# Splitting two more products of a polyphase convolution into half-width matmuls, with a staged third group

## The chip, the cores and the metric

One core of a Trainium2 chip. The metric is the time of one execution on the device in microseconds; the kernel before takes 896.56 us (median of 4 runs, 895.82 to 897.54). Its executions agree within some 0.3%. Differences of medians of 2 to 3 us are readable where the runs lie side by side, and smaller ones hardly.

## The reference

```python
# x (2, 4000, 512), w (15, 512, 1024), w_o (512, 512), all bf16
dil = 2; pad = (K - 1) * dil
xp = jnp.pad(x, ((0, 0), (pad, 0), (0, 0)))
h = sum(jnp.einsum('btc,cd->btd', xp[:, pad - i*dil : pad - i*dil + T, :], w[i]) for i in range(K))
z = jnp.tanh(h[..., :D]) * sigmoid(h[..., D:])
return z @ w_o
```
(The sum is written out as a loop there.) It is a causal convolution over time with 15 taps two steps apart, a gate, and an output projection.

## The kernel before

Time is cut into eight interleaved phases; four phases of one parity of one batch form a *supertile*. With three-multiplication tricks, nested, the convolution between four phases needs nine products (a, b, c, d, e, f, g, hh, ii) in place of sixteen; sums of inputs (U02 = U0 + U2 and so on) and sums of weights go in, sums and differences of the products come out. A *unit* is all nine products for one block of 128 output columns, one supertile and one half (tanh or sigmoid): 4 passes x 4 supertiles x 2 halves = 32 units. Only the first pass transposes and sums the inputs; it also writes them to DRAM, from where the later passes load them. Weights are summed anew for every pass. Work for later units (loads, sums, spills to DRAM) is attached to the products as *hooks*: a hook is issued behind the product whose index it carries.

A whole product is 16 matmuls of 501 columns (e has 12: a tap is missing). A *split* product applies the trick once more, along time: three groups of 8 matmuls of 251 columns.

```python
SPLIT = ("a", "c", "d", "f", "g", "ii")
...
wsl_pool:  bufs=33 + 2 * NSPL + 2      # weight slabs: 47 buffers
xin_pool:  bufs=(9 - NSPL) + 4         # natural inputs: 7
xh_pool:   bufs=NSPL                   # inputs in halves (odd "o", "m", "n"): 6
pcopy_pool 2, ctmp_pool 2, keep_pool 4, hpre_pool 2   # fp32 tiles of 501 columns
z_pool 6;  hsb_pool 2;  ps_pool 8 PSUM banks
...
def product(pn):                       # whole: 16 matmuls, N = 501, into one PSUM bank
    ...
def split_product(pn, dst):
    ps_o = ps_pool.tile([P, NH1], f32, ...)
    half_mms(ps_o, slabs2[pn], xt[n + "o"], True)              # group o: pair sums of weights
    u_h = hsb_pool.tile([P, NH1], f32, ...)
    nc.scalar.copy(u_h[:, :], ps_o[:, :])                      # must come before group m
    ps_e = ps_pool.tile([P, NH1], f32, ...)
    half_mms(ps_e, [sl[0], sl[2]], xt[n + "n"], True)          # group e
    V.tensor_tensor(dst[:, 1:NP1:2], ps_e[:, 1:NH1], u_h[:, 0:NKH], ALU.add)
    half_mms(ps_o, [sl[1], sl[3]], xt[n + "m"], False)         # group m, accumulates on ps_o
    nc.scalar.copy(dst[:, 0:NP1:2], ps_o[:, :])
...
def produce_halves(n):                 # first pass only
    nc.scalar.copy(to, nat[:, :, base + 1:base + 2 * XH:2])
    nc.scalar.copy(tm, nat[:, :, base:base + 2 * XH - 1:2])
    nc.gpsimd.memset(tn[:, :, 0:1], 0.0)
    sum_eng.tensor_tensor(tn[:, :, 1:XH], tm[:, :, 1:XH], to[:, :, 0:XH - 1], ALU.subtract)
    sum_eng.tensor_tensor(tm, tm, to, ALU.subtract)
...
for pi, pn in enumerate(PRODS):        # emit_unit
    if pn == "a":
        r["a_sb"] = to_sbuf("a", "a_sb")                       # split_product
    elif pn == "b":
        ps = product(pn)
        V.tensor_tensor(p1[:, K1], r["a_sb"][:, K1], ps[:, KSH], ALU.add)
        V.tensor_tensor(q1[:, K1], r["a_sb"][:, K1], ps[:, K1], ALU.add)
    ...                                # c .. ii in the same manner, act_out() for tanh, sigmoid
    for h in hooks.get(pi, []):        # loads, sums and spills for later units
        h()
...
# last unit: output projections as hooks (6, steps[0]), (7, steps[2]); steps[1], steps[3] after it
# zld_pool (loads of z for the output projection) 6, osb_pool 5
# weights of the next pass: half 0 in the last unit of a pass, half 1 in the first of the next
```

u_h is copied by ScalarE from the bank on which group m accumulates, so TensorE can't start group m before the copy is done.

## Time and profile before

| | before |
|---|---|
| time, median | 896.56 us; profiled span 894.3 us |
| matmuls, TensorE's granted clock | 6336, 0.998 |
| VectorE, ScalarE busy | 530.0 us (59%), 303.4 us (34%) |
| moved by DMA | 145.66 MB |
| one plain unit | 25.0 us |

The lines behind it stand in the prediction. Read them by the *starts* of TensorE's groups: what a pipelined engine takes for a group is the distance to the next start, not the duration printed beside it.

### The profile page before, as it was taken

The page shows a single profiled execution, that of the slowest core. Times are in us where ns is not written, and L with a number is a line of the kernel's source. Part 1 is how long each engine was busy: PE and PEld are TensorE (multiplying, and loading weights), DVE is VectorE, ACT ScalarE, POOL GpSimd, SP SyncE. Part 2 cuts the span into 40 slices and gives each one's busy share as a digit, 9 for nine tenths or more (in the row PEclk, how much of TensorE's full clock was granted, in tenths as well). Part 3 has the DMA queues.
Part 4 walks back from the last instruction along what each step waited for, and adds up shares of the span by engine and source line. Part 5 has one row for each costly group of instructions (what it writes and reads, how often), then busy time and mean ns, then how long its engine had stood idle before and what let it go on. Part 6 is the DMA issues. An engine that isn't in the chain of part 4 may idle for free.

```text
span 894.3 us, 16197 instructions
## 1 busy us (share of the span) xinstructions
PE 873.0 (98%) x6336; PEld 617.5 (69%) x6336; DVE 530.0 (59%) x1058; ACT 303.4 (34%) x625; POOL 27.7 (3%) x76
## 2 busy tenths in 40 slices
PE   6889999999999999999999999999999999999998
PEld 3356777777777777777777777777776676776674
DVE  3999596776975454455975454455974145244352
ACT  4435353632222222222222222222223423424334
POOL 8200000000000000000000000000000000000000
PEclk9999999999999999999999999999999999999999
DMA  9976656566948081636848081636937435435304
GB/s 226 314 196 232 143 196 171 174 231 171 240 131 248 14 251 40 203 102 177 237 127 264 15 249 42 202 103 177 243 105 239 135 119 179 121 105 167 99 2 126
DMA packets 138024, 145.66 MB, mean 163 GB/s; under 512 B 77276, under 2 KB 124700, under 8 KB 137948
## 3 DMA queue, kind: packets, MB, share of 16 engines
q1 hardware_dynamic: 136508, 140.70, 53.6%
q0 software_dynamic: 1440, 3.93, 1.7%
q8 instruction: 49, 0.80, 0.4%
q14 instruction: 27, 0.22, 0.1%
HBM read 99.25 MB, written 39.26 MB: 155 GB/s over the span
## 4 chain that ended last, share of the span: by engine, by line
PE 84%; DVE 10%; DMA 2%; issue 1%; ACT 1%; POOL 1%; SPq 0%; DVEq 0%; ACTq 0%; POOLq 0%
PE ps_b L341 11%; PE ps_hh L341 10%; PE ps_e L341 8%; PE po L481 6%; PE ps_c_o L354 6%; PE ps_d_o L354 6%; PE ps_f_o L354 5%; PE ps_a_o L354 5%; PE ps_ii_o L354 5%; PE ps_g_o L354 5%; PE ps_d_e L354 3%; PE ps_f_e L354 3%; PE ps_c_e L354 3%; PE ps_ii_e L354 3%; PE ps_g_e L354 3%; PE ps_a_e L354 3%
## 5 line engine op out<-in xcount | busy, mean ns | idle before, releaser
L341 PEld LDWEIGHTS <-wo_p 128*128 128x128 bf16 x1060 | 102.9, 97 | 110.0 <-issue 1.3
L354 PEld LDWEIGHTS <-wo_p 128*128 128x128 bf16 x1116 | 108.3, 97 | 16.7 <-issue 3.7
L341 PE MATMUL ps_b<-xU,wo_p 128*128 128x501 bf16 x512 | 113.8, 374 | 0.0
L341 PE MATMUL ps_e<-xU,wo_p 128*128 128x501 bf16 x384 | 86.9, 375 | 0.0
L341 PE MATMUL ps_hh<-xU,whh_p 128*128 128x501 bf16 x384 | 86.7, 375 | 0.0
L354 PEld LDWEIGHTS <-wii_p 128*128 128x128 bf16 x744 | 72.3, 97 | 16.9 <-issue 2.0
L354 PEld LDWEIGHTS <-wc_p 128*128 128x128 bf16 x744 | 72.1, 97 | 15.4 <-issue 0.3
L354 PEld LDWEIGHTS <-wg_p 128*128 128x128 bf16 x744 | 72.2, 97 | 9.0
L409 DVE TENSOR_TENSOR p<-a_sb,ps_b 128x500 f32<-128x500 f32 x32 | 21.6, 676 | 82.2 <-PE ps_b L341 81.8
L354 PEld LDWEIGHTS <-wf_p 128*128 128x128 bf16 x620 | 60.2, 97 | 13.6
L424 DVE TENSOR_TENSOR p<-d_sb,ps_e 128x500 f32<-128x500 f32 x32 | 21.6, 675 | 80.4 <-PE ps_e L341 76.0
L354 PE MATMUL ps_ii_o<-xU0123h,wii_p 128*128 128x251 bf16 x496 | 64.0, 271 | 1.8 <-ACT u_h L369 1.8
L354 PE MATMUL ps_c_o<-xU02h,wc_p 128*128 128x251 bf16 x496 | 64.0, 271 | 0.2 <-ACT u_h L369 0.2
L354 PE MATMUL ps_g_o<-xU01h,wg_p 128*128 128x251 bf16 x496 | 63.9, 271 | 0.0
L341 PEld LDWEIGHTS <-whh_p 128*128 128x128 bf16 x384 | 37.2, 97 | 38.2 <-DVE whh_p L164 0.4
L382 ACT ACTIVATE th<-H 128x500 bf16<-128x500 f32 x64 | 39.3, 620 | 50.4 <-DVE H L453 19.5
L386 ACT ACTIVATE sg<-H 128x500 bf16<-128x500 f32 x64 | 39.0, 620 | 37.9 <-DVE H L453 15.0
L481 PE MATMUL po<-wo_sb,zl 128*126 128x512 bf16 (+1 forms) x192 | 51.9, 379 | 0.0
L354 PE MATMUL ps_f_o<-xU13h,wf_p 128*128 128x251 bf16 x372 | 50.5, 271 | 0.0
L489 ACT CAST o_sb<-po 128x512 bf16<-128x512 f32 (+1 forms) x64 | 37.4, 586 | 32.6 <-PE po L481 29.3
L449 DVE TENSOR_TENSOR C<-g_sb,ps_hh 128x500 f32<-128x500 f32 x32 | 21.6, 674 | 44.6 <-PE ps_hh L341 44.5
L369 ACT COPY u_h<-ps_ii_o 128x251 f32<-128x251 f32 x31 | 11.4, 368 | 93.4 <-PE ps_ii_o L354 93.4
(122 smaller groups left out, 1253.5 us busy)
## 6 DMA issues: line engine op xcount, KB each, us to landing
xU<-xsp_U SPq DMA_DIRECT2D x36, 516.0 KB
wo_p<-in_w_dram SPq DMA_DIRECT2D x90, 128.0 KB
xU0h<-xsp_U0h SPq DMA_DIRECT2D x12, 756.0 KB
xU02h<-xsp_U02h SPq DMA_DIRECT2D x12, 756.0 KB
xU1h<-xsp_U1h SPq DMA_DIRECT2D x12, 756.0 KB
xU13h<-xsp_U13h SPq DMA_DIRECT2D x12, 756.0 KB
xU01h<-xsp_U01h SPq DMA_DIRECT2D x12, 756.0 KB
xU0123h<-xsp_U0123h SPq DMA_DIRECT2D x12, 756.0 KB
```

Source lines behind the costliest of these rows:

```text
L341: nc.tensor.matmul(ps[:, :], lhsT=slabs[pn][l][:, cc, hcols], rhs=xtile[:, cc, st:st + NP1], start=(idx == 0), stop=(idx == len(mm) - 1),)
L354: nc.tensor.matmul(ps[:, :], lhsT=taps[lam][:, cc, hcols], rhs=xtile[:, cc, st:st + NH1], start=(first and idx == 0), stop=(idx == len(mm) ...
L369: nc.scalar.copy(u_h[:, :], ps_o[:, :])
L382: nc.scalar.activation(th[:], H[:, K1], AF.Tanh)
L386: nc.scalar.activation(sg[:], H[:, K1], AF.Sigmoid)
L409: V.tensor_tensor(r["p1"][:, K1], r["a_sb"][:, K1], ps[:, KSH], ALU.add)
L424: V.tensor_tensor(r["p2"][:, K1], r["d_sb"][:, K1], ps[:, KSH], ALU.add)
L449: V.tensor_tensor(r["C0"][:, K1], r["g_sb"][:, K1], ps[:, KSH], ALU.add)
L481: nc.tensor.matmul(po[:ksz, :], lhsT=zs[dcp][:, k0:k0 + ksz], rhs=wo_sb[:, dcp, :], start=(dcp == 0), stop=(dcp == HC - 1),)
L489: nc.scalar.copy(o_sb[:ksz, :], po[:ksz, :])
```

## The change

The intent: b and hh are split as well (only e stays whole), so that each gives up a quarter of its matmul columns. Two products used to be read straight from PSUM and now become SBUF tiles; tiles are reused in place and pools shrink so that all fits. And the split is staged: group m of a product is issued after groups o and e of the next one, so that TensorE has work while ScalarE copies u_h.

```diff
-    SPLIT = ("a", "c", "d", "f", "g", "ii")
+    SPLIT = ("a", "b", "c", "d", "f", "g", "hh", "ii")
-    wsl_pool = ... bufs=33 + 2 * NSPL + 2          # 47
+    wsl_pool = ... bufs=33 + 2 * NSPL + 0          # 49, for 49 tiles
     xin_pool = ... bufs=(9 - NSPL) + 4             # 7 -> 5
     xh_pool = ... bufs=NSPL                        # 6 -> 8
-    pcopy 2, ctmp 2, keep 4, hpre 2, z 6
+    lng 3, sht 5, z 4                              # combinations in place
...
-        def split_product(pn, dst):
+        def split_stage_a(pn, dst):                # groups o and e, u_h, first addition
             ...
+            return ps_o
+        def split_stage_b(pn, dst, ps_o):          # group m and its copy
             half_mms(ps_o, [sl[1], sl[3]], xt[n + "m"], False)
             nc.scalar.copy(dst[:, 0:NP1:2], ps_o[:, :])
...
+        stage_a(PRODS[0])
+        for pi in range(1, NPR):
+            stage_a(PRODS[pi])
+            stage_b(pi - 1, PRODS[pi - 1])         # combinations and hooks are in stage_b
+        stage_b(NPR - 1, PRODS[NPR - 1])
...
-    xnat_pool = ... bufs=11                        # natural rows for the transposes
+    xnat_pool = ... bufs=9
+    WLEAD = 2                                      # two weight steps ahead of the first unit, not one
...
-            zld_pool bufs=6, osb_pool bufs=5
+            zld_pool bufs=5, osb_pool bufs=4
...                                                 # weights of the next pass, spread:
-                            add_hook(pi, nwsteps[0][pi])
-                        deferred_g = nwsteps[1]
+                            if pi < 5:
+                                add_hook(pi, nwsteps[0][pi])
+                        deferred_g = nwsteps       # the rest over the first two units of the next pass
...                                                 # last unit:
-                        add_hook(6, steps[0])
-                        add_hook(7, steps[2])
-                        pending_outproj = [steps[1], steps[3]]
+                        add_hook(5, steps[0])
+                        add_hook(6, steps[2])
+                        add_hook(7, steps[1])
+                        pending_outproj = [steps[3]]
```
(The schedule of input sums in the first pass, PROD_SCHED and HALF_SCHED, also moves: U23 is made earlier, U2 and U23 get their halves. In the first pass the last four weight steps of the second half also move, from the end of the first unit into the second.)

More of the change, by code (lines that the diff above doesn't have):

```diff
@@ L95 @@
     dram = ctx.enter_context(tc.tile_pool(name="dram", bufs=1, space=DRAM))
-    wsl_pool = ctx.enter_context(tc.tile_pool(name="wsl", bufs=33 + 2 * NSPL + 2))
+    wsl_pool = ctx.enter_context(tc.tile_pool(name="wsl", bufs=33 + 2 * NSPL + 0))
     xin_pool = ctx.enter_context(tc.tile_pool(name="xin", bufs=(9 - NSPL) + 4))
     xh_pool = ctx.enter_context(tc.tile_pool(name="xh", bufs=NSPL + XH_SPARE)) if NSPL else None
-    pcopy_pool = ctx.enter_context(tc.tile_pool(name="pcopy", bufs=2))
     hsb_pool = ctx.enter_context(tc.tile_pool(name="hsb", bufs=2)) if NSPL else None
-    ctmp_pool = ctx.enter_context(tc.tile_pool(name="ctmp", bufs=2))
-    keep_pool = ctx.enter_context(tc.tile_pool(name="keep", bufs=4))
-    hpre_pool = ctx.enter_context(tc.tile_pool(name="hpre", bufs=2))
+    lng_pool = ctx.enter_context(tc.tile_pool(name="lng", bufs=3))
+    sht_pool = ctx.enter_context(tc.tile_pool(name="sht", bufs=5))
     th_pool = ctx.enter_context(tc.tile_pool(name="th", bufs=4))
     sg_pool = ctx.enter_context(tc.tile_pool(name="sg", bufs=2))
-    z_pool = ctx.enter_context(tc.tile_pool(name="z", bufs=6))
+    z_pool = ctx.enter_context(tc.tile_pool(name="z", bufs=4))
     ps_pool = ctx.enter_context(tc.tile_pool(name="ps", bufs=8, space=PSUM))
@@ L372, in split_product @@
             V.tensor_tensor(dst[:, 1:NP1:2], ps_e[:, 1:NH1], u_h[:, 0:NKH], ALU.add)
+            return ps_o
+        def split_stage_b(pn, dst, ps_o):
+            n = XNAME[pn]
+            sl = slabs[pn]
             half_mms(ps_o, [sl[1], sl[3]], xt[n + "m"], False)
@@ L391, in act_out, with stage_a @@
                     nc.sync.dma_start(zsp[(dc, b, p, q)][:], zt[:])
-        def to_sbuf(pn, nm):
-            t = ftile(pcopy_pool, nm)
-            if pn in SPLIT and use_split:
-                split_product(pn, t)
+        SBUF_PRODS = {"a": sht_pool, "c": lng_pool, "d": sht_pool, "f": sht_pool, "g": lng_pool,
+                      "ii": sht_pool}
+        r = {}
+        pend = {}
+        def stage_a(pn):
+            is_split = pn in SPLIT and use_split
+            pool = SBUF_PRODS.get(pn, sht_pool if is_split else None)
+            if pool is None:
+                r[pn] = product(pn)
+                return
+            t = ftile(pool, pn + "_sb")
+            r[pn] = t
+            if is_split:
+                pend[pn] = split_stage_a(pn, t)
             else:
@@ L399, in to_sbuf @@
                 nc.scalar.copy(t[:, ALLC], ps[:, ALLC])
-            return t
-        r = {}
-        for pi, pn in enumerate(PRODS):
-            if pn == "a":
-                r["a_sb"] = to_sbuf("a", "a_sb")
-            elif pn == "b":
-                ps = product(pn)
-                r["p1"] = ftile(keep_pool, "p1")
-                V.tensor_tensor(r["p1"][:, K1], r["a_sb"][:, K1], ps[:, KSH], ALU.add)
-                r["q1"] = ftile(ctmp_pool, "q1")
-                V.tensor_tensor(r["q1"][:, K1], r["a_sb"][:, K1], ps[:, K1], ALU.add)
-            elif pn == "c":
-                if "c" in SPLIT and use_split:
-                    ps = to_sbuf("c", "c_sb")
-                else:
-                    ps = product(pn)
-                r["A1"] = ftile(keep_pool, "A1")
-                V.tensor_tensor(r["A1"][:, K1], ps[:, K1], r["q1"][:, K1], ALU.subtract)
-            elif pn == "d":
-                r["d_sb"] = to_sbuf("d", "d_sb")
-            elif pn == "e":
-                ps = product(pn)
-                r["p2"] = ftile(keep_pool, "p2")
-                V.tensor_tensor(r["p2"][:, K1], r["d_sb"][:, K1], ps[:, KSH], ALU.add)
-                r["q2"] = ftile(ctmp_pool, "q2")
-                V.tensor_tensor(r["q2"][:, ALLC], r["d_sb"][:, ALLC], ps[:, ALLC], ALU.add)
-            elif pn == "f":
-                if "f" in SPLIT and use_split:
-                    ps = to_sbuf("f", "f_sb")
-                else:
-                    ps = product(pn)
-                r["B1"] = ftile(keep_pool, "B1")
-                V.tensor_tensor(r["B1"][:, ALLC], ps[:, ALLC], r["q2"][:, ALLC], ALU.subtract)
-                H0 = ftile(hpre_pool, "H0")
-                V.tensor_tensor(H0[:, K1], r["p1"][:, K1], r["B1"][:, KSH], ALU.add)
@@ new lines, in stage_b @@
+        def stage_b(pi, pn):
+            if pn in pend:
+                split_stage_b(pn, r[pn], pend.pop(pn))
+            if pn == "b":
+                r["p1"] = ftile(lng_pool, "p1")
+                V.tensor_tensor(r["p1"][:, K1], r["a"][:, K1], r["b"][:, KSH], ALU.add)
+                V.tensor_tensor(r["a"][:, K1], r["a"][:, K1], r["b"][:, K1], ALU.add)
+            elif pn == "c":
+                V.tensor_tensor(r["c"][:, K1], r["c"][:, K1], r["a"][:, K1], ALU.subtract)
+            elif pn == "e":
+                r["p2"] = ftile(sht_pool, "p2")
+                V.tensor_tensor(r["p2"][:, K1], r["d"][:, K1], r["e"][:, KSH], ALU.add)
+                V.tensor_tensor(r["d"][:, ALLC], r["d"][:, ALLC], r["e"][:, ALLC], ALU.add)
+            elif pn == "f":
+                V.tensor_tensor(r["f"][:, ALLC], r["f"][:, ALLC], r["d"][:, ALLC], ALU.subtract)
+                H0 = ftile(sht_pool, "H0")
+                V.tensor_tensor(H0[:, K1], r["p1"][:, K1], r["f"][:, KSH], ALU.add)
@@ L436, in emit_unit @@
                 act_out(0, H0)
-                H2 = ftile(hpre_pool, "H2")
-                V.tensor_tensor(H2[:, K1], r["A1"][:, K1], r["p2"][:, K1], ALU.add)
-                act_out(2, H2)
                 V.tensor_tensor(r["p1"][:, K1], r["p1"][:, K1], r["p2"][:, K1], ALU.add)
-                r["s"] = r["p1"]
-                V.tensor_tensor(r["A1"][:, K1], r["A1"][:, K1], r["B1"][:, K1], ALU.add)
-                r["s3"] = r["A1"]
-            elif pn == "g":
-                r["g_sb"] = to_sbuf("g", "g_sb")
-            elif pn == "hh":
-                ps = product(pn)
-                r["C0"] = ftile(ctmp_pool, "C0")
-                V.tensor_tensor(r["C0"][:, K1], r["g_sb"][:, K1], ps[:, KSH], ALU.add)
-                r["qg"] = ftile(ctmp_pool, "qg")
-                V.tensor_tensor(r["qg"][:, K1], r["g_sb"][:, K1], ps[:, K1], ALU.add)
-                H1 = ftile(hpre_pool, "H1")
-                V.tensor_tensor(H1[:, K1], r["C0"][:, K1], r["s"][:, K1], ALU.subtract)
-                act_out(1, H1)
-            elif pn == "ii":
-                if "ii" in SPLIT and use_split:
-                    ps = to_sbuf("ii", "ii_sb")
-                else:
-                    ps = product(pn)
-                r["C1"] = ftile(ctmp_pool, "C1")
-                V.tensor_tensor(r["C1"][:, K1], ps[:, K1], r["qg"][:, K1], ALU.subtract)
-                H3 = ftile(hpre_pool, "H3")
-                V.tensor_tensor(H3[:, K1], r["C1"][:, K1], r["s3"][:, K1], ALU.subtract)
-                act_out(3, H3)
@@ new lines, in stage_b @@
+                V.tensor_tensor(r["p2"][:, K1], r["c"][:, K1], r["p2"][:, K1], ALU.add)
+                act_out(2, r["p2"])
+                V.tensor_tensor(r["c"][:, K1], r["c"][:, K1], r["f"][:, K1], ALU.add)
+            elif pn == "hh":
+                C0 = ftile(sht_pool, "C0")
+                V.tensor_tensor(C0[:, K1], r["g"][:, K1], r["hh"][:, KSH], ALU.add)
+                V.tensor_tensor(r["g"][:, K1], r["g"][:, K1], r["hh"][:, K1], ALU.add)
+                V.tensor_tensor(C0[:, K1], C0[:, K1], r["p1"][:, K1], ALU.subtract)
+                act_out(1, C0)
+            elif pn == "ii":
+                V.tensor_tensor(r["ii"][:, K1], r["ii"][:, K1], r["g"][:, K1], ALU.subtract)
+                V.tensor_tensor(r["ii"][:, K1], r["ii"][:, K1], r["c"][:, K1], ALU.subtract)
+                act_out(3, r["ii"])
@@ L494 @@
     USE_DMAT = True
-    PROD_SCHED = [(0, "U0"), (0, "U2"), (0, "U1"), (0, "U3"), (4, "U02"), (5, "U13"), (6, "U01"),
-                  (7, "U23"), (8, "U0123")]
-    HALF_SCHED = [(4, "U0"), (5, "U02"), (5, "U1"), (6, "U13"), (7, "U01"), (8, "U0123")]
+    PROD_SCHED = [(0, "U0"), (0, "U2"), (0, "U1"), (0, "U3"), (4, "U02"), (4, "U23"), (5, "U13"),
+                  (6, "U01"), (8, "U0123")]
+    HALF_SCHED = [(4, "U0"), (4, "U2"), (5, "U02"), (5, "U1"), (6, "U13"), (7, "U01"), (8, "U23"),
+                  (8, "U0123")]
     HALF_SCHED = [(pi, n) for (pi, n) in HALF_SCHED if n in XSPLIT]
@@ L501 @@
     es0 = ExitStack()
-    xnat_pool = es0.enter_context(tc.tile_pool(name="xnat", bufs=11))
+    xnat_pool = es0.enter_context(tc.tile_pool(name="xnat", bufs=9))
     wts, wsteps = make_weight_steps(0, nc.vector, nc.gpsimd, defer_pairs=True)
@@ L507 @@
     XLEAD = 2
+    WLEAD = 2
     for pi in range(XLEAD):
         xsteps[pi]()
-    wsteps[0][0]()
+    for pi in range(WLEAD):
+        wsteps[0][pi]()
     deferred_g = None
@@ L517 @@
             nc.sync.dma_start(wo_sb[:], w_o.rearrange("(dc p) e -> p dc e", p=P))
-            zld_pool = ctx.enter_context(tc.tile_pool(name="zld", bufs=6))
-            osb_pool = ctx.enter_context(tc.tile_pool(name="osb", bufs=5))
+            zld_pool = ctx.enter_context(tc.tile_pool(name="zld", bufs=5))
+            osb_pool = ctx.enter_context(tc.tile_pool(name="osb", bufs=4))
         pending_outproj = []
@@ L536 @@
                             add_hook(pi, xsteps[pi + XLEAD])
-                        if pi + 1 < NPR:
-                            add_hook(pi, wsteps[0][pi + 1])
+                        if pi + WLEAD < NPR:
+                            add_hook(pi, wsteps[0][pi + WLEAD])
                         if pi >= GLAG:
                             add_hook(pi, wsteps[1][pi - GLAG])
+                if dc == 0 and si == 0 and hf == 1:
                     for pj in range(NPR - GLAG, NPR):
-                        add_hook(NPR - 1, wsteps[1][pj])
+                        add_hook(pj - (NPR - GLAG), wsteps[1][pj])
                 if hf == 0 and dc == 0:
@@ L575 @@
                             add_hook(pi, nxs["steps"][pi])
-                            add_hook(pi, nwsteps[0][pi])
-                        deferred_g = nwsteps[1]
+                            if pi < 5:
+                                add_hook(pi, nwsteps[0][pi])
+                        deferred_g = nwsteps
                     else:
                         steps = make_outproj_steps(b, p, state["z"])
-                        add_hook(6, steps[0])
-                        add_hook(7, steps[2])
-                        pending_outproj = [steps[1], steps[3]]
+                        add_hook(5, steps[0])
+                        add_hook(6, steps[2])
+                        add_hook(7, steps[1])
+                        pending_outproj = [steps[3]]
                 if hf == 0 and si == 0 and dc > 0 and deferred_g is not None:
-                    for pi in range(NPR):
-                        add_hook(pi, deferred_g[pi])
-                    deferred_g = None
+                    for pi in range(5, NPR):
+                        add_hook(pi - 5, deferred_g[0][pi])
+                    for pi in range(5):
+                        add_hook(pi + 4, deferred_g[1][pi])
+                    late_g, deferred_g = deferred_g[1], None
+                if hf == 1 and si == 0 and dc > 0:
+                    for pi in range(5, NPR):
+                        add_hook(pi - 5, late_g[pi])
                 if last_pass and hf == 0 and pending_outproj:
```

## The prediction

> **What bounds the kernel now.** I read the page first, then the TensorE timeline of one plain unit, then what TensorE waited for, then the busy times unit by unit. A unit is one pass over the nine products a, b, c, d, e, f, g, hh, ii for one 128-column block, one supertile and one half (tanh or sigmoid); there are 4 x 4 x 2 = 32 of them. The page:
>
> ```profile
> PE 873.0 (98%) x6336; PEld 617.5 (69%) x6336; DVE 530.0 (59%) x1058; ACT 303.4 (34%) x625; POOL 27.7 (3%) x76
> PEclk9999999999999999999999999999999999999999
> ...
> PE 84%; DVE 10%; DMA 2%; issue 1%; ACT 1%; POOL 1%; SPq 0%; DVEq 0%; ACTq 0%; POOLq 0%
> ```
>
> TensorE is busy nearly always, at full clock, and is 84% of the chain that ended last. Busy time of a pipelined engine proves little, so I look at starts. The TensorE timeline of one unit:
>
> ```profile
> 462.03 3.56 PE L341 MATMUL ps_b<-xU,wo_p 128*128 128x501 bf16 x16
> 465.43 1.03 PE L354 MATMUL ps_c_o<-xU02h,wc_p 128*128 128x251 bf16 x8
> 466.30 1.03 PE L354 MATMUL ps_c_e<-xU02h,wc_p 128*128 128x251 bf16 x8
> 467.17 1.03 PE L354 MATMUL ps_c_o<-xU02h,wc_p 128*128 128x251 bf16 x8
> 468.04 1.03 PE L354 MATMUL ps_d_o<-xU1h,wd_p 128*128 128x251 bf16 x8
> ...
> 478.41 2.71 PE L341 MATMUL ps_hh<-xU,whh_p 128*128 128x501 bf16 x12
> 480.96 1.01 PE L341 MATMUL ps_hh<-xU,wo_p 128*128 128x501 bf16 x4
> 481.80 1.03 PE L354 MATMUL ps_ii_o<-xU0123h,wii_p 128*128 128x251 bf16 x8
> ```
>
> Each row starts where the one before has issued its last matmul. A whole product b takes 465.43 - 462.03 = 3.40 us (16 matmuls, 212 ns each); hh takes 481.80 - 478.41 = 3.39 us. A split product takes 468.04 - 465.43 = 2.61 us (24 half-width matmuls, 109 ns each). The windows view, cut at unit boundaries (columns: window, length, busy time of PE, PEld, DVE, ACT and POOL):
>
> ```profile
> 11.00:52.40 41.40, 35.43 (x176) 15.69 (x174) 36.08 (x75) 17.24 (x22) 14.75 (x25) 0.96 1.04 293
> 52.40:77.40 25.00, 24.97 (x198) 17.87 (x197) 23.55 (x53) 13.86 (x22) 0.73 (x6) 1.00 0.53 159
> 77.40:105.50 28.10, 26.16 (x199) 19.01 (x197) 20.76 (x36) 11.16 (x22) 0.66 (x5) 1.00 0.79 212
> ...
> 308.20:333.20 25.00, 25.00 (x190) 18.26 (x189) 12.47 (x23) 6.83 (x17) 0.00 (x0) 1.00 0.69 213
> 433.20:458.20 25.00, 25.00 (x191) 18.27 (x189) 25.00 (x66) 6.58 (x16) 0.00 (x0) 1.00 0.72 197
> ```
>
> A plain unit is 25.0 us = 6 x 2.61 + 2 x 3.40 + 2.55 (e, 12 matmuls), so it is the matmul stream and nothing else; VectorE and ScalarE are half idle beside it. Two kinds of units are different: the first one (41.4 us) and the first of each later pass (433.2 here), where VectorE is busy all 25.0 us with weight sums, yet TensorE keeps its pace. All that TensorE waited for in the whole run is 17 us:
>
> ```profile
> PE pt L231 <- DMA xn<-in_x_dram: 7.2, 4, 3.3
> PE ps_ii L341 <- DVE wii_p L164: 3.1, 1, 3.1
> PE ps_g L341 <- DVE wg_p L164: 2.8, 3, 1.7
> PE ps_a_o L354 <- ACT u_h L369: 2.1, 3, 1.1
> PE ps_ii_o L354 <- ACT u_h L369: 1.8, 1, 1.8
> ```
>
> So the time is the sum of matmul columns plus some 17 us, most of it in the first unit.
>
> **What the Trainium skill says.** "TensorE: Matmul & The Clock Gate", section Back-to-back issue gap, gives N/2.4 + 2.5 ns for a warm matmul: 107 ns for 251 columns and 211 ns for 501. The trace has 109 and 212, so it agrees; the same section's sustained figure of about 131 ns for N=512 does not fit this trace. What matters: a half-width matmul really costs half, and the weight loads (97 ns each, 69% of the span) stay under it. The page's section Part 2 says that only weight loads are pulled ahead and matmuls stay in program order, so one matmul that waits for ScalarE stops all; the five u_h waits above agree. "VectorE: DVE Perf Modes", section The TRN2 errata, gives (N+151)/0.96 ns for an fp32 tensor_tensor, 678 ns at N=500. The trace has 676 ns with one operand in PSUM and 679 with both in SBUF, so moving b and hh to SBUF should not change the cost of the combining additions.
>
> **The change part by part.**
> 1. Products b and hh are split like the six others: 16 matmuls of 501 columns become 24 of 251. 3.40 - 2.61 = 0.79 us each, twice a unit, in 31 units (the first unit doesn't split): 31 x 2 x 0.79 = 49.0 us off the stream. All of it lies on the path.
> 2. In exchange each of the 62 new splits adds two ScalarE copies (368 and some 385 ns) and one VectorE addition (0.41 us): 47 us of ScalarE, 25 us of VectorE. Per plain unit VectorE goes to some 13.3 of 23.4 us, ScalarE to some 8.4. Beside the stream; nothing on the path.
> 3. Inputs U2 and U23 now get halves: per supertile four ScalarE copies of 1.04 us and four VectorE subtractions of 0.68 us, all in the first pass (16.6 and 10.9 us in total). Weight pair sums rise by 8 a pass, from 60 to 68 VectorE operations of about 0.36 us: 12 us over the run. VectorE in total: 530 + 25 + 11 + 12 = 578 us, 68% of the new span. ScalarE: 303 + 47 + 17 = 367 us, 43%.
> 4. Loads and spills of the two inputs grow from 516 to 756 KB, in 12 loads and 4 spills each: 16 x 2 x 0.24 = 7.7 MB on 145.66 MB. The mean goes from 163 to some 181 GB/s; slices of the page reach 314. Hidden.
> 5. Staging: the third group of a split product now runs after the first two groups of the next product. That gives the u_h copy one more product, some 1.7 us of slack. The u_h waits are 2.1 + 1.8 + 0.2 = 4.1 us; I expect nearly all to go.
> 6. The weight sums of a pass are spread. By my count of the additions, before, some 16, 41 and 3 fall into the last unit of the old pass and the first two of the new; after, 12, 34 and 22. The unit with 34 has 13.3 + 34 x 0.36 = 25.5 us of VectorE work in 23.4, so VectorE falls some 2 us behind and carries that on. Two u_h buffers and eight PSUM banks absorb about 6 us (the third group of a product comes 7.8 us after its first copy two products earlier, less 1.5 us of copy and addition). The weight pool has no spare buffer left, so sums and loads wait for the product that frees one, some 2.6 us each, in a lightly loaded unit. I allow 1 us for all of this and for the smaller output-projection pools.
> 7. Start-up. Before the second supertile begins to run freely (105.5 us), VectorE is busy 81 us; I add 5.4 for halves, 3 for pair sums, 1.6 for additions. The natural input pool shrinks from 7 to 5 buffers, and the first unit uses all nine natural tiles: U01 can only be made when U13 is freed by product f, so g waits for at least one 1.23 us sum. Against it, the new order asks for one input step less ahead of each product. I put the net at 4 us longer.
> Sum: 896.6 - 49.0 - 4.1 + 1 + 4 = 848.5; I say 848.
>
> **The rivals.** (A) VectorE becomes the bound in some units, the first three and the first of each pass. For it: 25.00 of 25.00 us busy at 433.2, 36.08 of 41.40 in the first unit. Against it: TensorE didn't slow at all at 433.2, and the sums are now spread. It would give back 3 us per pass change and 6 to 10 at the start, so 855 to 865. (B) The removed buffers take the place of the wait: input, weight and combine tiles turn over later, and transfers on the one queue sit behind a wait for a buffer. For it: weights 49 for 49 tiles, halves 8 for 8. Against it: a load issued in one unit is needed a whole unit, 23 us, later. If it held, every supertile would lose 1 to 2 us: 865 to 880. (C) The extra stage does more than I think and start-up waits shrink as well: 830 to 842, where 830 is 896.6 - 49.0 with all 17.4 us of waits gone. For it: the g and ii waits (2.8 and 3.1 us) are VectorE order, which the change rearranges. Against it: 7.2 us of the 17 are the first loads, which it doesn't touch. (D) Half-width matmuls in unbroken rows meet a limit of the weight loads (97 under 109 ns leaves 12). Against it: c and d already run 48 in a row at 109 ns.
>
> **Range and chances.** The 49 us are counted and I trust them to 1 us. The rest, +1 from a sum of -4 and +5, could be -7 (C, mildly) or +14 (A in full). So 838 to 862. Slower or the same within 2% needs 30 us of new waits, more than any of my sums finds.
>
> **What would show it.** Right: 6336 + 62 x 8 = 6832 matmuls; ps_b and ps_hh groups at 24 half-width matmuls in 2.61 us; plain units of 23.4 us; u_h waits of TensorE under 1 us; VectorE near 578 us, ScalarE near 367. Wrong: plain units longer than 23.6 us (B or D), TensorE waiting more than 3 us at 220, 410 or 600 us, near pass changes (A), or a first unit longer than 47 us.

## The result, and the profile after

The changed kernel takes **856.09 us** (median of 8 runs, 853.34 to 858.1) against 897.07 us of the kernel before in the same rounds: a ratio of 0.9542 (95% interval 0.9528 to 0.9556). Ratios here are the mean time of one kernel's fast runs over that of the other's of the same rounds, so not quite the ratio of the medians that are quoted. The profiled spans are 894.3 and 854.7 us, at clocks of 0.998 and 0.995.

The page after, its line of engines:

```profile
PE 827.0 (97%) x6832; PEld 667.4 (78%) x6832; DVE 577.3 (68%) x1168; ACT 364.9 (43%) x768; POOL 28.4 (3%) x84
```

6832 matmuls, as counted; VectorE and ScalarE gained 47 and 61 us and the kernel became 40 us shorter, which is what "beside the stream" means here. The TensorE timeline of a plain unit after, around b:

```profile
489.20 1.03 PE L352 MATMUL ps_b_o<-xU2h,wb_p 128*128 128x251 bf16 x8
490.07 1.03 PE L352 MATMUL ps_b_e<-xU2h,wo_p 128*128 128x251 bf16 x8
490.94 1.03 PE L352 MATMUL ps_a_o<-xU0h,wo_p 128*128 128x251 bf16 x8
491.81 1.03 PE L352 MATMUL ps_c_o<-xU02h,wc_p 128*128 128x251 bf16 x8
```

Two things are to be seen: b comes in groups that start 0.87 us apart, 109 ns a matmul, so three of them make 2.61 us; and between groups e of b and o of c stands the third group of a, the staging. This unit runs from 487.46 to 510.87, so 23.41 us in place of 25.0.

The windows view after, for the first three units and for a change of pass (window, length, then busy us with the number of instructions for PE, PEld, DVE, ACT and POOL, granted clock, DMA share, GB/s):

```profile
0.00:52.20 52.20, 39.40 (x204) 19.39 (x205) 36.84 (x76) 24.95 (x32) 24.42 (x51) 0.97 0.81 250
52.20:74.50 22.30, 22.30 (x206) 18.63 (x205) 22.16 (x56) 12.43 (x22) 0.85 (x7) 1.00 0.61 128
74.50:106.00 31.50, 27.73 (x222) 22.19 (x220) 29.30 (x53) 20.08 (x36) 0.77 (x6) 0.95 0.86 264
...
417.00:440.60 23.60, 23.57 (x206) 19.82 (x205) 23.44 (x60) 7.35 (x19) 0.00 (x0) 1.00 0.86 227
440.60:464.00 23.40, 23.40 (x206) 19.80 (x205) 20.73 (x49) 8.71 (x22) 0.00 (x0) 1.00 0.65 219
```

At this change of pass, the second, VectorE is full again (23.44 of 23.60 us) and TensorE still loses only 0.2 us. At the first one it loses more: unit 9 takes 25.18 us, with a u_h wait of 1.6 us ahead of group m of ii. In units 2 and 3 VectorE is just as full, and there unit 3 takes 31.5 us, of which TensorE is busy 27.7. Not all of these 27.7 us are at full speed, as the clock of 0.95 says: from 84.8 to 88.2 us the granted clock is half, and matmuls of 251 columns start 208 to 212 ns apart.

```profile
84.64 1.69 PE L352 MATMUL ps_a_o<-xU0h,wo_p 128*128 128x251 bf16 x8 [1.28 <-ACT u_h L367]
...
86.75 1.76 PE L352 MATMUL ps_d_o<-xU1h,wd_p 128*128 128x251 bf16 x8
```

Up to unit 4 the kernel before has one such stretch (47.3 to 50.7 us) and the changed one two (the other from 40.5 to 43.9). Whether the second one costs anything is answered under 7 below.

TensorE's waits after (what waited for what: us in total, times, longest):

```profile
PE pt L229 <- DMA xn<-in_x_dram: 6.6, 4, 3.3
PE ps_ii_o L352 <- ACT u_h L367: 2.7, 3, 1.6
PE ps_g L339 <- DVE xU L267: 2.2, 1, 2.2
PE po L469 <- DVE zt L391: 2.2, 3, 1.7
PE ps_a_o L352 <- ACT u_h L367: 1.3, 1, 1.3
PE ps_b_o L352 <- ACT u_h L367: 1.2, 2, 0.6
```

The u_h waits are still there (6.4 us with two short ones not shown, against 4.1 before), and two of over 2 us are new: g for a sum of inputs in the first unit, and the last output projections for zt (0.2 us before).

To say where the 49 us of saved stream went, the span is cut at TensorE's first matmul of certain units, in both traces (and in that of the first experiment, which is the change with six splits):

| stretch | before | six splits, e1 | after | stream saved | given back |
|---|---|---|---|---|---|
| start to unit 4 | 105.5 | 102.9 | 106.0 | 3.2 | 3.7 |
| units 4 to 7 (the first pass up to its last unit) | 102.0 | 101.7 | 98.5 | 6.3 | 2.8 |
| units 8 to 26 | 477.3 | 475.3 | 447.0 | 30.0 | -0.3 |
| units 27 to 31 (with output projections) | 166.4 | 167.2 | 158.5 | 7.9 | 0.0 |
| unit 32 and the end | 43.1 | 44.4 | 44.7 | 1.6 | 3.2 |
| sum | 894.3 | 891.4 | 854.7 | 49.0 | 9.4 |

"Stream saved" is 1.58 us (2 x 0.79) for each unit but the first; "given back" is after - (before - saved). From unit 8 to unit 31 the gain arrives whole. The 9.4 us sit at the start, in the first pass and at the end.

In the first pass the u_h waits can be followed in ScalarE's timeline; the number in brackets is the idle time ahead and what ended it:

```profile
133.66 1.03 ACT L274 COPY xU01h<-xU 128x1008 bf16<-128x1008 bf16 x1 [1.29 <-DVE xU L267]
134.61 1.03 ACT L275 COPY xU01h<-xU 128x1008 bf16<-128x1008 bf16 x1
135.54 1.03 ACT L274 COPY xU23h<-xU 128x1008 bf16<-128x1008 bf16 x1
136.48 1.03 ACT L275 COPY xU23h<-xU 128x1008 bf16<-128x1008 bf16 x1
137.42 0.36 ACT L367 COPY u_h<-ps_b_o 128x251 f32<-128x251 f32 x1
```

and in TensorE's:

```profile
137.83 1.03 PE L352 MATMUL ps_b_o<-xU2h,wo_p 128*128 128x251 bf16 x8 [0.60 <-ACT u_h L367]
```

The copy of u_h is 0.36 us of work but stands in order behind four half copies, and these behind a VectorE sum. The six waits of this kind between 106 and 205 us sum to 2.7 us, nearly the 2.8 given back there.

### The profile page after: what moved, and what is told of

Same layout as the page of the kernel before. It is cut to its first block, busy times and chain, and to the rows that moved or that the text cites.

```text
span 854.7 us, 17399 instructions
## 1 busy us (share of the span) xinstructions
PE 827.0 (97%) x6832; PEld 667.4 (78%) x6832; DVE 577.3 (68%) x1168; ACT 364.9 (43%) x768; POOL 28.4 (3%) x84
## 2 busy tenths in 40 slices
DMA packets 125742, 153.60 MB, mean 180 GB/s; under 512 B 77276, under 2 KB 108316, under 8 KB 125660
## 4 chain that ended last, share of the span: by engine, by line
PE 80%; DVE 11%; DMA 4%; issue 2%; ACT 2%; POOL 0%; ACTq 0%; SPq 0%; DVEq 0%; POOLq 0%
PE ps_e L339 8%; PE ps_c_o L352 6%; PE po L469 6%; PE ps_a_o L352 5%; PE ps_f_o L352 5%; PE ps_d_o L352 5%; PE ps_b_o L352 5%; PE ps_ii_o L352 5%; PE ps_g_o L352 5%; PE ps_hh_o L352 5%; DMA wo_p<-in_w_dram 4%; PE ps_c_e L352 3%; PE ps_a_e L352 3%; PE ps_b_e L352 3%; PE ps_hh_e L352 3%; PE ps_f_e L352 3%
## 5 line engine op out<-in xcount | busy, mean ns | idle before, releaser
L352 PEld LDWEIGHTS <-wc_p 128*128 128x128 bf16 x744 | 72.3, 97 | 11.4 <-issue 2.1
L370 DVE TENSOR_TENSOR f_sb<-ps_f_e,u_h 128x250 f32<-128x250 f32 x31 | 12.9, 417 | 93.6 <-PE ps_f_e L352 90.6
L352 PEld LDWEIGHTS <-whh_p 128*128 128x128 bf16 x620 | 60.1, 97 | 8.6 <-issue 1.1
L352 PE MATMUL ps_hh_o<-xU23h,whh_p 128*128 128x251 bf16 x372 | 50.6, 271 | 0.9 <-ACT u_h L367 0.9
L377 ACT COPY d_sb<-ps_d_o 128x251 f32<-128x251 f32 x31 | 12.1, 390 | 84.9 <-PE ps_d_o L352 84.9
L370 DVE TENSOR_TENSOR c_sb<-ps_c_e,u_h 128x250 f32<-128x250 f32 x31 | 12.9, 415 | 45.8 <-PE ps_c_e L352 45.6
L469 PEld LDWEIGHTS <-zl 128*126 128x126 bf16 (+1 forms) x192 | 24.1, 125 | 14.6
L352 PE MATMUL ps_a_o<-xU0h,wo_p 128*128 128x251 bf16 x248 | 32.6, 274 | 1.3 <-ACT u_h L367 1.3
L429 DVE TENSOR_TENSOR f_sb<-f_sb,d_sb 128x501 f32<-128x501 f32 x32 | 21.8, 680 | 17.9 <-ACT f_sb L377 17.5
L352 PE MATMUL ps_c_e<-xU02h,wc_p 128*128 128x251 bf16 x248 | 32.5, 273 | 0.9 <-ACT ii_sb L377 0.9
```

Of the source, the lines that this page charges most:

```text
L352: nc.tensor.matmul(ps[:, :], lhsT=taps[lam][:, cc, hcols], rhs=xtile[:, cc, st:st + NH1], start=(first and idx == 0), stop=(idx == len(mm) ...
L429: V.tensor_tensor(r["f"][:, ALLC], r["f"][:, ALLC], r["d"][:, ALLC], ALU.subtract)
L469: nc.tensor.matmul(po[:ksz, :], lhsT=zs[dcp][:, k0:k0 + ksz], rhs=wo_sb[:, dcp, :], start=(dcp == 0), stop=(dcp == HC - 1),)
```

## The experiments

The theory: the stream's saving is real everywhere; staging removes u_h waits; the losses are VectorE's load at the start and smaller pools. Its rivals, by part of the change, stand in each expectation. Calls differ in chip; the kernel before took 897.15 us (e1 to e4), 896.24 (e5, e7, e8, e9), 897.16 (e10, b2, b4) and 897.26 (b5, its fast runs) beside them. In the last call one run of the kernel before took 1858.96 us; it is not among the fast runs. All the results were correct.

**e1: six splits, the rest of the change kept.**

```diff
-    SPLIT = ("a", "b", "c", "d", "f", "g", "hh", "ii")
+    SPLIT = ("a", "c", "d", "f", "g", "ii")
```

> The changed kernel with b and hh taken out of the split list again; staging, new hook order, merged combine pools and new output-projection order stay. Theory (the gain is the matmul stream: 0.79 us for each of 62 new splits, 49 us; the rest of the change is worth a few us either way): plain units are back at 25.0 us, time 891 to 900. Rival (the new order and the staging removed waits and are a good part of the gain): plain units of 24.0 us or a time under 880.

Measured: 892.96 us (891.93 to 894.48), ratio 0.9951 (0.9932 to 0.997). Plain units are 24.99 us. So all that isn't the split is worth some 4 us by itself, and splitting b and hh is worth 892.96 - 856.09 = 37 us net of the 49. The table above shows where the other 12 went: the start, 102.9 - 3.2 = 99.7 expected and 106.0 measured, loses 6.3; units 4 to 7 lose 3.1; the end 1.9; units 8 to 26 1.7, and units 27 to 31 win 0.8 back. (With six splits the pool of natural inputs has 7 buffers again, since its size is computed from the number of splits, and U2 and U23 need no halves; these can't be told apart from the split itself in this run.)

**e2: group m straight after its own groups o and e, as before.**

```diff
-        stage_a(PRODS[0])
-        for pi in range(1, NPR):
+        for pi in range(NPR):
             stage_a(PRODS[pi])
-            stage_b(pi - 1, PRODS[pi - 1])
-        stage_b(NPR - 1, PRODS[NPR - 1])
+            stage_b(pi, PRODS[pi])
```

> The changed kernel with the third group of a split product put back directly behind its first two; b and hh stay split. Theory (staging only removes the few u_h waits, 4 us by the prediction): plain units stay at 23.4 us, time 856 to 863, TensorE waits on u_h grow by some us. Rival (with three splits in a row the u_h copy no longer fits in the 0.87 us of the second group, so staging is what makes the split of b and hh pay): plain units of 24 us or more, time over 868.

Measured: 868.43 us (867.83 to 872.39), ratio 0.9688. Plain units are 23.67 us and 24.0 us in turn. TensorE's waits, and the timeline at one of them:

```profile
PE ps_hh_o L352 <- ACT u_h L367: 4.4, 12, 0.4
```

```profile
536.36 1.03 PE L352 MATMUL ps_hh_e<-xU23h,whh_p 128*128 128x251 bf16 x8
536.57 0.62 ACT L385 ACTIVATE th<-p 128x500 bf16<-128x500 f32 x1 [0.49 <-DVE p L434]
537.10 0.35 ACT L367 COPY u_h<-ps_hh_o 128x251 f32<-128x251 f32 x1
537.50 0.60 PE L352 MATMUL ps_hh_o<-xU23h,whh_p 128*128 128x251 bf16 x4
```

Group e gives ScalarE 0.87 us. A tanh of 0.62 us came first, the copy ended at 537.45, and group m, due at 536.36 + 0.87 = 537.23, started at 537.50. Staging is worth 12 us, not 4 (the edit also moves the combinations and hooks ahead by a product, so this is the staged order as a whole): in the kernel before such waits were rare (4.1 us in the whole run), and with eight splits and no staging one comes in nearly every unit, at hh, which wasn't split before. The theory's 856 to 863 us missed. The rival was nearer: the time is just over its 868, and every second plain unit takes the 24.0 us that it named.

**e3: the output projections of the last unit where they were.**

```diff
-                        add_hook(5, steps[0])
-                        add_hook(6, steps[2])
-                        add_hook(7, steps[1])
-                        pending_outproj = [steps[3]]
+                        add_hook(6, steps[0])
+                        add_hook(7, steps[2])
+                        pending_outproj = [steps[1], steps[3]]
```

> The changed kernel with the output-projection steps of the last unit where they were before: two inside it, two behind it. Theory (the 8 us by which the prediction missed are in part at the end: with one step left behind product ii, TensorE waits 1.7 us and some short ones for the last z and the final copies start later; last unit and what follows it cost 3.3 us more than the stream says): 852.5 to 854.5, the last unit 38.0 us or less instead of 39.7. Rival (the end is set by the chain of the last z and the stores whatever the order): within 0.5 us of the changed kernel.

Measured: 855.56 us (854.38 to 856.46), ratio 0.9532: the same. The waits for zt are gone, and another has taken their place:

```profile
PE po L469 <- DMA zl<-zsp: 1.8, 2, 1.3
```

zl are the stored z of the earlier passes, loaded into the pool that went from 6 buffers to 5. From the start of the last unit to the end it takes 43.9 us (after 44.7). The order alone isn't the cause.

**e4: one input step more ahead of the first unit.**

```diff
-    XLEAD = 2
+    XLEAD = 3
```

> The changed kernel with the inputs of the first supertile issued three products ahead instead of two. Theory (in the staged order a hook comes one product later, so in the first unit the transposes of U1 and U3 come just before products d and e, which wait for them; 4 us of gaps there): first unit 39 us instead of 41.8 and time 852.5 to 854.5; the 2.2 us wait of g for U01 stays, because that is the input pool of 5. Rival (the first unit is bound by VectorE, 35.8 of 41.8 us busy, and by the first loads): the gaps move to another product and the first unit stays at 41 to 42 us.

Measured: 855.7 us (854.47 to 855.74), ratio 0.9531. The first unit is 37.7 us in place of 41.8, 4.1 less, and yet unit 4 starts at 104.3 in place of 106.0: the first unit began 0.4 us later, and units 2 and 3 give back 1.9 us (55.7 in place of 53.8).

**e5: the second half copy of U2 and U23 on GpSimd in place of ScalarE.**

```diff
-            nc.scalar.copy(tm, nat[:, :, base:base + 2 * XH - 1:2])
+            if n in ("U2", "U23"):
+                nc.gpsimd.tensor_copy(tm, nat[:, :, base:base + 2 * XH - 1:2])
+            else:
+                nc.scalar.copy(tm, nat[:, :, base:base + 2 * XH - 1:2])
```

> The changed kernel; of the two strided copies that make the halves of U2 and U23, one goes from ScalarE to the idle GpSimd. Theory (in the first pass the new halves fill ScalarE's queue with 1.04 us copies, and the u_h copies that TensorE waits for stand behind them: 0.7 to 0.8 us twice for each supertile from 130 us on): the u_h waits between 106 and 205 us fall from 3.7 us to under 1.5 and the four units there from 98.5 to 96 us; time 852 to 854.5. Rival (VectorE is late and ScalarE only waits for it; GpSimd reading SBUF delays VectorE further): these units stay at 98 us or grow.

Measured: 863.52 us (863.08 to 864.59), ratio 0.9634: worse. The copy took 1.04 us on ScalarE; on GpSimd that of U2 took 1.08 to 2.07 us and that of U23 3.01 to 4.12. The timeline of GpSimd:

```profile
46.52 3.78 POOL L276 COPY xU23h<-xU 128x1008 bf16<-128x1008 bf16 x1 [11.75 <-DVE xU L267]
```

and of VectorE beside it:

```profile
48.75 0.67 DVE L436 TENSOR_TENSOR p<-p,p 128x500 f32<-128x500 f32 x1
50.34 0.68 DVE L280 TENSOR_TENSOR xU23h<-xU23h 128x1004 bf16<-128x1004 bf16 x1 [0.92 <-POOL xU23h L276]
```

VectorE runs additions of two SBUF tiles without a gap until 49.4, and the GpSimd copy ends 0.9 us after that. The Trainium skill, "SBUF — State Buffer", section Who interferes with whom, says that a VectorE instruction with two SBUF inputs contends with a GpSimd instruction that reads SBUF. The 3.78 us under a row of such additions fit that, but this trace doesn't settle it: the copies of U2 that took 1.08 to 1.13 us ran beside VectorE operations with two SBUF inputs as well. What makes the U23 copies slow stays open. Unit 2 now starts at 57.4 in place of 52.2, and units 4 to 7 take 99.4 us (98.5). Their six u_h waits sum to 3.6 us (0.9 twice at c, the others 0.4 to 0.5), where after has 2.7 (the 3.7 of the expectation is not in the trace), so they didn't go. The run doesn't settle whether ScalarE's occupancy alone makes those waits, since the copy that was moved became a new one.

**e7: the weight sums of a pass where they were** (half 0 in the last unit of the old pass, half 1 in the first of the new; the weight pool stays at 49).

```diff
-                            if pi < 5:
-                                add_hook(pi, nwsteps[0][pi])
-                        deferred_g = nwsteps
+                            add_hook(pi, nwsteps[0][pi])
+                        deferred_g = nwsteps[1]
...
+                    for pi in range(NPR):
+                        add_hook(pi, deferred_g[pi])
+                    deferred_g = None
```

> The changed kernel with the weight loads and sums of a pass back in the old places: all of the first half in the last unit of the old pass, all of the second half in the first unit of the new one; the pool stays at 49 tiles for 49. Theory (prediction part 6: spreading the sums keeps VectorE from falling behind; 41 of 60 sums then fall in one unit that is now 23.4 us and holds 13.7 us of other VectorE work): the first two units of passes 2 to 4 lose 1 to 3 us each, time 858 to 864. Rival (VectorE's backlog is absorbed by the buffers as it was before): within 1 us of the changed kernel, 855 to 857.

Measured: 867.1 us (864.87 to 867.65), ratio 0.9667. That is more than the theory's 858 to 864. The first units of the second, third and fourth pass take 25.7, 28.3 and 25.4 us, the units after them 25.2, 24.6 and 24.9. The worst in the windows view (417.00 to 440.60 after took 23.60):

```profile
419.00:447.40 28.40, 25.28 (x207) 20.65 (x206) 25.72 (x66) 8.15 (x21) 0.00 (x0) 0.94 0.73 195
```

Of its 28.4 us, 1.7 are a stretch of half clock (434.1 to 437.6 us) after a u_h wait of 3.1 us. Over the run, TensorE waits 11.4 us for u_h ahead of the third group of c. Spreading the sums is worth 11 us. The kernel before had this schedule and lost only 2.6 us by it (the units after the first of a pass took 25.79, 26.25 and 25.52 us, the others 24.99), so it is a thing that eight splits need, not a gain by itself: rival A of the prediction was a real danger, and this part of the change met it.

**e8: XLEAD 3, and U01 made ahead of U13.**

```diff
-    XLEAD = 2
+    XLEAD = 3
-                            add_hook(pi, xsteps[pi + XLEAD])
+                            add_hook(pi, xsteps[(0, 1, 2, 3, 4, 6, 5, 7, 8)[pi + XLEAD]])
```

> The kernel of the run with inputs three products ahead, and in addition U01 is made before U13 in the first unit, so that it takes the buffer of U02 and needs not wait for product f to free U13. Theory A (the 2 us wait of product g is the pool of 5): that wait goes, first unit 35.5 us, and 2 us stay gained at 106 us: time 853 to 854. Theory B (up to the second supertile VectorE is the bound, some 88 us busy of 95; a wait removed in the first unit comes back in the next two, as in the run before, where 4.1 us of gain in the first unit had become 1.7 us at 104 us): first unit shorter, but third unit starts and ends within 1 us of 71.7 and 104.3 us, time 855 to 856.

Measured: 854.84 us (854.07 to 855.64), ratio 0.9535. The wait of g for U01 is gone; hh now waits 3.0 us for its weight sums, and unit 4 starts at 105.2. The wait was replaced, not removed.

**e9: e3, and 6 buffers for zl** (room for it made by freeing the identity tile after the first pass).

```diff
     # e3, and
-            zld_pool = ctx.enter_context(tc.tile_pool(name="zld", bufs=5))
+            zld_pool = ctx.enter_context(tc.tile_pool(name="zld", bufs=6))
-    ident = const.tile([P, P], bf16, name="ident")
+    idp = es0.enter_context(tc.tile_pool(name="idp", bufs=1))   # closed after the first pass
+    ident = idp.tile([P, P], bf16, name="ident")
```

> The kernel with the old order of the last output projections, and 6 instead of 5 buffers for the stored z that they load (the space comes from the identity matrix, moved to the pool that is freed after the first pass). Theory (with the old order TensorE waited 0.6 and 1.5 us for these loads, because the third load of a step must wait until the step before frees its buffers; the pool cut from 6 to 5 is what took the tail's gain away): those waits go, the last unit is 37.6 to 38.2 us, time 853 to 854. Rival (the loads are late because of the queue in front of them): waits on these loads stay and the time is 855 to 856.

Measured: 852.49 us (852.3 to 853.41), ratio 0.9511. The waits of the output projections for zl and for zt are both gone, and from the start of the last unit to the end it takes 850.5 - 809.0 = 41.5 us, which is 43.1 - 1.6: the whole 3.2 us given back at the end are accounted for. The sixth buffer with the new order wasn't run.

**e10: 6 natural inputs in the first pass** (paid for with 5 row buffers in place of 9).

```diff
-    xin_pool = ctx.enter_context(tc.tile_pool(name="xin", bufs=(9 - NSPL) + 4))
+    xin2_pool = ...bufs=1                              # later passes
+    xin_pool = es0.enter_context(... name="xin", bufs=6)   # freed after the first pass
-    xnat_pool = ... bufs=9
+    xnat_pool = ... bufs=5
     # and wo_sb allocated in the last pass alone, ident freed after the first
```

> The changed kernel with a sixth buffer for the natural inputs of the first pass (the space: these buffers are freed after the first pass, later passes have one of their own, the output weights come in late, row buffers 9 to 5). Theory (the 3.7 us lost in the units from 106 to 205 us are a burst on VectorE: idle for some 3.7 us between 111 and 122 us while the input sum U02 waits for a buffer, then busy without a break from 122.5 to 145 us; the sixth buffer lets the sum start earlier): these four units fall from 98.5 us to 95.5 to 97, and the 2.2 us wait of product g in the first unit goes; time 850 to 854. Rival (the lists of hooks set the time of these sums, not the buffers): the four units stay at 98 to 98.7 us.

Measured: 854.98 us (853.97 to 856.82), ratio 0.9532. Units 4 to 7 take 97.2 us (98.5), just outside of what was expected. The first unit is 37.2 us, 4.6 less, units 2 and 3 take 5.3 us more, and unit 4 starts at 106.8. The sixth buffer is worth 1.3 us in units 4 to 7. At the start no gain is left, but there the row buffers went from 9 to 5 at the same time, and the two can't be told apart.

**b2: e10, the tail of e9 with 5 buffers for o_sb, and XLEAD 3, to see whether the gains add.**

```diff
     # e10, e3 and
-    XLEAD = 2
+    XLEAD = 3
-            zld_pool bufs=5, osb_pool bufs=4
+            zld_pool bufs=6, osb_pool bufs=5
```

> Sixth input buffer, inputs three ahead, old tail order with six load buffers and five store buffers. Theory: gains add, 848 to 851: the stream of 826 us with some 22 us of start, VectorE bursts and end. Rival (the first 105 us are bound by VectorE's work, not by buffers): start of the fourth unit still at 104 us or later, time 851 to 852.5.

Measured: 857.02 us (855.33 to 859.8), ratio 0.9557. A miss: with 5 row buffers and one input step more ahead, the transposes wait 11.2 us for rows, and the first unit takes 46.3 us.

**b4: e9 and e8 together.**

```diff
     # e9 and
-    XLEAD = 2
+    XLEAD = 3
-                            add_hook(pi, xsteps[pi + XLEAD])
+                            add_hook(pi, xsteps[(0, 1, 2, 3, 4, 6, 5, 7, 8)[pi + XLEAD]])
```

> Both small repairs together, on five input buffers: old order of the last output projections with six load buffers, and inputs three ahead with U01 before U13. If their gains add (3.4 us and 1 us against the changed kernel): 851 to 852.5. If start-up work that moves comes back later: 852.5, as with the tail alone.

Measured: 851.79 us (851.14 to 852.6), ratio 0.9496. Unit 4 starts at 105.1; nearly all of the gain is e9's, and the 0.7 us between the two medians are within the noise.

**b5: b4, and all copies of the transposed inputs on ScalarE** (before, every second one on VectorE).

```diff
-                        pe_rows(t, xn, k0, ksz, pt, s_, s_)
+                        pe_rows(t, xn, k0, ksz, pt, s_, 0)
```

> The kernel with both small repairs, and the four copies of transposed rows per first-supertile input that VectorE and ScalarE shared now all go to ScalarE: some 3.3 us of work leaves VectorE before 52 us. Theory (up to the start of the fourth unit the sum of VectorE's work is the bound: 88.3 us busy in every version, start at 104.3 to 106.8 us however the waits lay): the fourth unit starts 2 to 3.5 us earlier than 105.1 us; time 848 to 850. Rival (start-up is a chain of transposes, sums and loads, and VectorE is only busy beside it): start within 1 us of 105.1 us or later, time 851 to 854, since a ScalarE copy takes 0.58 us and a VectorE copy 0.41.

Measured: 850.72 us (850.01 to 852.05), ratio 0.9485 (0.9472 to 0.9499). That is the lowest median, but not clear of b4's 0.9496 (0.9482 to 0.951), so no gain over b4 is shown. VectorE's work up to unit 4 fell from 88.3 us to 85.8, and unit 4 starts at 105.0, as in b4. The windows view of its units 2 and 3:

```profile
50.20:73.30 23.10, 23.10 (x214) 19.39 (x213) 22.88 (x59) 12.50 (x23) 0.84 (x7) 1.00 0.29 74
73.30:105.00 31.70, 25.21 (x214) 20.55 (x212) 29.50 (x53) 19.90 (x36) 0.76 (x6) 1.00 0.86 265
```

VectorE is busy 52.4 of the 54.8 us here, and the work that was taken from it lay ahead of 50 us, where it had gaps. A theory of the start as VectorE's total work falls; what remains is a stretch from 50 us to 99 us in which VectorE is full, and which no run with eight splits took work from: units 2 and 3 together take 53.8 us after and 54.8 here.

## Why the prediction was right

Predicted 848.0 us, range 838 to 862; measured 856.09. The mechanism and the main term held, and the terms beside it were mis-sized by 8 us.

1. *The stream, -49.0.* Right: 6832 matmuls, b in three groups of 0.87 us, plain units of 23.41 us (predicted 23.4), and the 24 units from 8 to 31 are (477.3 + 166.4) - (447.0 + 158.5) = 38.2 us shorter, where 24 x 1.58 = 37.9 was counted. The loads of weights, now 78% of the span, cost nothing, so rival D is out.
2. *and 3. The work of the other engines.* Right: VectorE 577.3 us (578), ScalarE 364.9 (367); the combining additions, now with both operands in SBUF, take 0.67 to 0.68 us as before. Beside the stream in the plain units; not so in the first pass, see 7.
4. *Transfers.* Right in size (153.60 MB, 180 GB/s), and hidden.
5. *Staging, -4.1.* Wrong twice. The u_h waits didn't go (4.1 before, 6.4 after, where under 1 was expected): the remaining ones lie in the first pass and once at a change of pass, where ScalarE's copy comes late by the work queued ahead of it (at the change of pass a tanh that waits for VectorE until 251.07), and a stage more doesn't cover that. And the value of staging is 12 us (e2): the prediction took the waits of six splits for the waits of eight. As the change has both, the sum was off by the 4.1 us that didn't go and the 2.3 us by which the waits grew.
6. *Weight sums and smaller pools, +1.* The weight sums cost no more than that: first units of a pass take 25.18, 23.6 and 23.58 us and the second ones 23.41, so 2.1 us are lost in three changes of pass, where the kernel before lost 2.6. Without the spreading it would have been 11 us more (e7). The prediction's count of the sums before was a little off: by the trace some 20, 40 and 0 fall into the three units, not 16, 41 and 3; after it is 12 or 13, 35 or 36 and 20, near its 12, 34 and 22. The output-projection pool, however, is the mis-sized term: the end gave back 3.2 us, and e3 with e9 show that the sixth zl buffer and the old order remove all of it.
7. *The start, +4.* Right in size, 3.7 us, though partly by luck: it was argued from the input pool and from VectorE. e10 gave the sixth input buffer, e4 the earlier input, e8 the other order, b5 less work for VectorE; each shortened the first unit or removed the wait that was named, and none moved unit 4 by more than 1.7 us. The loss lies in units 2 and 3: 53.1 us before, 53.8 after, where the stream alone gives 50.0. What sets the end of unit 3 can be read in the traces. Its last wait is that of f for an addition on VectorE:

```profile
93.70 1.03 PE L352 MATMUL ps_f_o<-xU13h,wf_p 128*128 128x251 bf16 x8 [0.68 <-DVE a_sb L370]
```

This addition stands in a row of VectorE operations without a gap since 80.66, so f starts 13.04 us after the row does, and unit 4 follows 12.32 us after f, without a wait. In e3, e4 and b5 it is again 13.04 and 12.32 us, although their rows start at 80.60, 78.92 and 79.65. The half clock isn't the cause: e3 has no such stretch in unit 3, and its unit 3 takes 31.54 us where after takes 31.53. So at the end of unit 3 TensorE waits for VectorE's order of work; that less work in this row would bring unit 4 forward wasn't run.
8. *Not foreseen: units 4 to 7, 2.8 us.* The prediction counted the halves of U2 and U23 as work beside the stream. In these units they come in a burst, and ScalarE holds u_h behind them for 0.6 us at a time. The six waits are 2.7 of the 2.8 us. One more input buffer returned 1.3 us (e10).

By place: the net of the terms beside the stream was predicted as -4.1 + 1 + 4 = +0.9 us and is 3.7 + 2.8 - 0.3 + 0.0 + 3.2 = +9.4.

Of the rivals, A (VectorE as the bound) is true of the first pass and of one wait of 1.6 us at the first change of pass: the measured time lies in its range of 855 to 865 us, but the 3 us for each change of pass that it counted didn't come. B (buffers that take the place of the wait) is true of the end and of 1.3 us in units 4 to 7, and of nothing in the 24 units between; C is out.

## What to carry to other kernels

Where one engine is the bound, count its stream by starts and trust that count: here it was right to 1% over 24 units, and what had to be found was a few waits at the start, at the end and in bursts. A part of a change can be worth much more with the rest of it than alone (staging 4 us by the old waits, 12 us in the new kernel; spreading the sums 11 us), so judge it by taking it out of the whole. And a wait that is removed while another engine is full further on comes back: e4 took 4.1 us off the first unit and kept 1.7, e10 (with fewer row buffers) took 4.6 off and kept none.

## What the Trainium skill lacked or had wrong

- "TensorE: Matmul & The Clock Gate", section Back-to-back issue gap: the simple formula, which the page gives for single matmuls, holds in a real stream of load and matmul pairs (109 ns at 251 columns, 212 ns at 501); the "sustained" figure of about 131 ns at 512 columns, said to be the one for real kernels, was not seen: the output projections' matmuls of 512 columns start 215 to 216 ns apart.
- The same page, Part 3, section The mechanism: one list there lets weight loads overlap matmuls only when the row group differs (the text above the list also allows a load into a background buffer, so the section doesn't agree with itself). Here loads of 128 x 128 take 97 ns each, matmuls of the whole array start every 109 ns, and a plain unit holds 23.41 us; one after the other they would need 206 ns a pair.
- "GPSIMD Engine Reference", section 4.1 Engine selection, calls elementwise work with one input roughly line-rate. A strided bf16 copy of 128 x 1008 (e5) took 1.08 to 1.13 us three times, 2.07 once and 3.01 to 4.12 us four times, against 1.04 us on ScalarE, always beside VectorE operations with two SBUF inputs. The page names a contention elsewhere; what separates the fast copies from the slow ones no run here shows.
- No page that I read has what a copy from PSUM between two accumulation groups costs when its engine has other work in the queue: with one group of 0.87 us to cover it, 0.26 or 0.59 us of TensorE in a plain unit (e2, at hh).
